# A recorded program becomes a graph that a list scheduler emits; maximum of x and part of a leaky rectifier go to ScalarE

## The chip, the cores and the metric

The kernel runs on one core of a Trainium2 chip. The metric is the device time of one execution in microseconds (us), the median of several; lower is better. Engines are named as in the profile: PE (TensorE matmul), PEld (its weight loads), DVE (VectorE), ACT (ScalarE), POOL (GpSimd), SP (SyncE, which issues DMAs). A name with a q is an engine's DMA queue or sequencer.

## What is computed

Four stages in a row, all in float32 accuracy:

```python
scores = q @ k^T / 8 - log(448)              # 4 batches x 12 heads, 448 positions, 64 wide
x   = sigmoid(scores) @ v                    # then heads side by side: 1792 tokens x 768
h   = x @ w_in;  g = h - tanh(h)             # layer 1, 768 -> 2048
x2  = g @ w_out                              # layer 2, 2048 -> 768
h2  = x2 @ w_in2                             # layer 3, 768 -> 2048
g2  = max(h2, 0) + alpha * min(h2, 0)        # leaky rectifier, alpha per column
out = g2 @ w_out2                            # layer 4, 2048 -> 768
```

## The kernel before

**Matmuls.** Every float32 operand is split into two float16 halves, high and low (`hi = f16(x*s)`, `lo = f16(x*s - hi)`); a product is three passes, hi*hi, hi*lo, lo*hi. All matmuls have 448 columns. The tokens are in two halves (`sb` 0 and 1) of 896. The attention runs in 12 groups `g`; each has seven units `u` of scores (`scores`) and seven of values (`values`, float32 matmuls), the values two steps behind the scores. Layers 1 and 2 (`product`) have 1152 matmuls of 128x128x448 each; layer 1 visits `sb` 0 four columns ahead of `sb` 1. Layers 3 and 4 use seven products in place of eight (`SEQ = (1, 2, 6, 5, 7, 4, 3)`, Strassen-like sums of blocks) and have 1008 matmuls each, 504 for a half. In layer 3 each half has four rounds `q`, each of seven units of 18 matmuls (`matmuls_in`).

**Buffers.** 51 slots of 128x896 float32 in SBUF are taken and given back by `alloc` and `release`, the longest free one first. PSUM has four tiles of two banks, ps0 to ps3. In the attention ps0 to ps2 go round for scores and ps3 collects the values. Layers 1 and 2 go round all four. In layer 3, products 1, 6, 7 and 4 gather in ps0 or ps1 (by round), product 2 in ps2, products 5 and 3 in ps3; what stands in ps0 or ps1 is copied out after product 1, after 6 and after 7, and read by the rectifier after 4.

**Side work.** Each of the weights' 64 units (768 columns) comes from HBM as 64-bit words into one of four staging tiles (POOL queue), three DVE instructions make float32 of it (`words`), layers 3 and 4 add and subtract blocks (`quarter`), the halves are made (`halves_of`: high on ACT or DVE, low on DVE), and a POOL-queue DMA stores them to scratch in HBM (`to_scratch`). SP fetches them from there when they are near their use. Between layers a scale is found: a maximum over a tile (`absmax` for x on DVE; from layer 1 on ACT sums squares), over the partitions on POOL, then seven small DVE instructions (`scale_jobs`), and the activations are split with it (`split_job`, `in_jobs`, `out_jobs`).

**What sets the order.** The program is emitted in the order in which the Python runs, and each engine executes its own instructions in that order. The class `Engine` keeps a rough clock per engine; `bg` pops jobs (or a step of the weights' conversion) into the DVE and ACT streams while DVE's clock is behind PE's. A low half is kept back until the next `settle`. The rectifier of layer 3 is `finish`: DVE adds the PSUM tile to the copy, two DVE `tensor_scalar` make `alpha*min`, one DVE instruction adds `max`, ACT squares the result with a running sum. Product 4 (`tail_in`) uses two ACT Relus and two DVE instructions instead.

Of the kernel before, what the change touches and what calls it, by code (L numbers as in the profile page):

```python
# [19 lines left out]
T2 = 2 * S  # L34
# [3 lines left out]
UN = 6  # L38
NU = KD * KF // UN

# [7 lines left out]
DEPTH = 5  # L48
# [6 lines left out]
LAG = 4  # L55


class Engine:
# [3 lines left out]
    def __init__(self, tc, raw, pe=None):  # L62
        self.tc, self.raw, self.pe, self.t = tc, raw, pe, 0.0

    def __getattr__(self, op):
        f = getattr(self.raw, op)

        def call(*args, **kw):
            if "dma" in op or op in ("memset", "partition_all_reduce"):
                return self.tc.keep_in_program_order(f(*args, **kw))  # L70
            out, args = args[0], args[1:]
            used = [a for a in (out, *args) if hasattr(a, "space")]
            n = int(np.prod((args[0] if op == "tensor_reduce" else out).shape[1:]))
            if op == "matmul":
                part = args[0].shape[0] * args[0].shape[1] / 16384
                self.t += part * n * (1.68e-3 if args[0].dtype == F32 else 0.421e-3) + (0.01 if part < 1 else 0.0)
            else:
                if any(a.space == bass.MemoryType.PSUM for a in used):
                    self.t = max(self.t, self.pe.t)
                    rate = 1.04e-3  # L80
                else:
                    rate = 0.52e-3 if op == "tensor_scalar" else 1.04e-3
                self.t += n * (0.83e-3 if op == "activation" else rate) + (0.26 if op == "activation" else 0.16)
            return self.tc.keep_in_program_order(f(out, *args, **kw))  # L84

        return call
# [3 lines left out]
def body(ctx: ExitStack, tc, qkd, vd, w1, w2, w3, w4, al, out):  # L90
    nc = tc.nc
    PE = Engine(tc, nc.tensor)
    V, A = Engine(tc, nc.vector, PE), Engine(tc, nc.scalar, PE)
    G, SP = Engine(tc, nc.gpsimd), Engine(tc, nc.sync)
# [5 lines left out]
    scratch = {(m, pr, q): dr_pool.tile([128, 2 * UN * 128], F16, name=f"scr{m}_{pr}_{q}")  # L100
               for m in (2, 3) for pr in range(1, 8) for q in range(NQ)}
    scratch.update({u: dr_pool.tile([128, 2 * UN * 128], F16, name=f"scr_{u}") for u in range(2 * NU)})
    slots = [sb_pool.tile([128, T2], F32, name=f"slot{i}") for i in range(NSLOT)]
    stage = [sb_pool.tile([128, UN * 128, 2], I32, name=f"stage{i}") for i in range(NSTAGE)]
# [4 lines left out]
    sc = sb_pool.tile([128, 8, 8], F32, name="sc")  # L109
    sci = sc.bitcast(I32)  # L110
    pst = [ps_pool.tile([128, 2, 512], F32, name=f"ps{i}") for i in range(4)]

    free = list(slots)

    def alloc():
        return free.pop(0)

    def release(t):
        free.append(t)
# [6 lines left out]


    wd = (w1, w2, w3, w4)
    wslot = {}
    loaded = [0]  # L130

    def load_unit(queue=G):
        i = loaded[0]
        if i < 4 * NU:
            src = wd[i // NU][i % NU].bitcast(I32)
            queue.dma_start(out=stage[i % NSTAGE].rearrange("p a b -> p (a b)"), in_=src)
            loaded[0] += 1

    def words(i, w):
        st = stage[i % NSTAGE]  # L140
        lo, hi = st[:, :, 0], st[:, :, 1]
        V.tensor_scalar(w, hi, 3, 0x3FFFFFFF, ALU.logical_shift_left, ALU.bitwise_and)
        yield
        V.scalar_tensor_tensor(w, hi, -0x40000000, w, ALU.bitwise_and, ALU.bitwise_or)
        yield
        V.scalar_tensor_tensor(w, lo, 29, w, ALU.logical_shift_right, ALU.bitwise_or)
        load_unit()
        yield

    def pair_of(s):  # L150
        return s.bitcast(F16)[:, 0:2 * UN * 128].rearrange("p (a c) -> p a c", a=2)

    late = []

    def settle():
        while late:
            late.pop(0)()

    def halves_of(hi, lo, src, scale, then):

        def low():
            V.scalar_tensor_tensor(lo, src, scale, hi, ALU.mult, ALU.subtract)
            then()

        if V.t + 0.4 < A.t:
            V.tensor_scalar(hi, src, scale, None, ALU.mult)
        else:
            A.activation(hi, src, AF.Copy, scale=scale)
        settle()
        late.append(low)  # L170

    def to_scratch(key, src, scale, then):
        t = alloc()
        v = pair_of(t)

        def stored():
            G.dma_start(out=scratch[key], in_=t.bitcast(F16)[:, 0:2 * UN * 128])
            release(t)
            then()

        halves_of(v[:, 0], v[:, 1], src, scale, stored)

    def counted(w):
        def f():
            release(w)
            nconv[0] += 1
        return f

    def conv():
        for i in range(2 * NU):  # L190
            w = alloc()
            yield from words(i, w.bitcast(I32)[:, 0:UN * 128])
            to_scratch(i, w[:, 0:UN * 128], SW, counted(w))
            yield
        for m in (2, 3):
            for q in range(NQ):
                yield from quarter(m, q)


    def quarter(m, q):  # L200
        def unit(b):
            s = alloc()
            yield from words(NU * m + 4 * q + b, s.bitcast(I32)[:, 0:UN * 128])
            f.append(s)

        def fl(s):
            return s[:, 0:UN * 128]

        def put(pr, s, last, scale=SW2):
            to_scratch((m, pr, q), fl(s), scale, lambda: release(s) if last else None)  # L210

        f = []
        yield from unit(0)
        yield from unit(1)
        a21, a22 = f
        r = alloc()
        V.tensor_tensor(fl(r), fl(a21), fl(a22), ALU.add)
        yield
        put(5, r, False)
        yield  # L220
        put(4, a22, True, -SW2)
        yield
        yield from unit(2)
        a11 = f[2]
        V.tensor_tensor(fl(r), fl(r), fl(a11), ALU.subtract)
        yield
        put(6, r, False)
        V.tensor_tensor(fl(a21), fl(a11), fl(a21), ALU.subtract)
        yield
        put(7, a21, True)  # L230
        yield
        put(1, a11, True)
        yield
        yield from unit(3)
        a12 = f[3]
        V.tensor_tensor(fl(r), fl(a12), fl(r), ALU.subtract)
        yield
        put(3, r, True)
        yield
        put(2, a12, True)  # L240
        yield
        settle()
        prepared.add((m, q))
        nconv[0] += 4

    prepared = set()
    nconv = [0]
    conv_gen = conv()
    reserve = [0]

    def conv_step(force=False):
        if nconv[0] >= 4 * NU or (not force and len(free) <= reserve[0]):
            return False
        next(conv_gen, None)
        V.t += 0.06
        return True

    def weight(m, n):
        load_units(m * NU + n // UN + 1)
        v = wslot[m, n // UN].bitcast(F16)[:, 0:2 * UN * 128]  # L260
        return v.rearrange("p (a k c) -> p a k c", a=2, k=UN)[:, :, n % UN, :]

    taken = [0]

    def load_units(upto):
        while taken[0] < min(upto, 3 * NU):
            i = taken[0]
            src = i if i < 2 * NU else i - NU
            while nconv[0] <= src:
                settle() if late else conv_step(True)  # L270
            t = alloc()
            SP.dma_start(out=t.bitcast(F16)[:, 0:2 * UN * 128], in_=scratch[src])
            wslot[divmod(i, NU)] = t
            taken[0] += 1

    jobs = []
# [10 lines left out]
    def flush():  # L287
        while jobs:
            jobs.pop(0)()

    def scale_jobs(g, n, f0=1.0, f1=1.0, root=None, exp=ACT_EXP, sw=SW):
        c = sc[:, g]
        ci = sci[:, g]

        def first():
            V.tensor_reduce(c[:, 0:1], mx[:, g, 0:n], AX.X, ALU.max)
            G.partition_all_reduce(c[:, 1:2], c[:, 0:1], 128, bass_isa.ReduceOp.max)  # L300
            return 0.1

        def second():
# [11 lines left out]
            return 0.5  # L315

        return first, second

    def unit_jobs(g):

        c, ci = sc[:, g], sci[:, g]
# [660 lines left out]
```

## Time and profile before

| what | value |
|---|---|
| runs: median (lowest to highest of 3) | 985.47 us (983.61 to 986.0) |
| the profiled execution: span, first to last instruction | 981.4 us; of its own time only this span is given |
| PE busy | 948.3 us |
| DVE, ACT, POOL busy | 772.2, 512.8, 84.9 us |
| matmuls | 5280, of them 4320 in the layers |

A row of the timeline reads: start, time covered, engine, line, operation, out<-in, count, and in brackets the idle time before and what ended it. In the kernel before, all engines' instructions have line 84 and POOL's DMAs line 70, since a helper records them, so rows are told apart by names and shapes: `slot` an SBUF slot, `ps` a PSUM tile, `sc` the scales, `stage` the staging tiles, `scr` scratch in HBM. A stretch's row gives its length and each engine's busy time and count, the granted TensorE clock (1.00 is 2.4 GHz, 0.50 is 1.2 GHz), the DMA share and GB/s.

### The profile page before, as it was taken

Reading aid. Unit: us, or ns where it says so; the run is one execution under the profiler, and the core shown is the slowest. Engines: PE = TensorE matmul, PEld = TensorE weight load, DVE = VectorE, ACT = ScalarE, POOL = GpSimd, SP = SyncE. Lnnn points to the kernel's source line nnn. Section 1 sums busy time; section 2 is a strip of 40 time slices with the busy share of each in tenths; the row PEclk is TensorE's granted clock in tenths of the full one; section 3 lists DMA queues with packets and bytes.
Section 4 is the critical chain, followed back from the end, with each engine's and each line's share of the span. In section 5 each row is a group of like instructions: output and inputs, shape, how many; then the busy total and the mean of one; then the engine's idle time right before and its main releaser. Section 6 shows DMA issues by size and latency. Waiting matters only on the chain. (4 is left out here: it accounts for less than half of the span.)

```text
span 981.4 us, 13376 instructions
## 1 busy us (share of the span) xinstructions
PE 948.3 (97%) x5280; PEld 465.3 (47%) x5280; DVE 772.2 (79%) x949; ACT 512.8 (52%) x628; POOL 84.9 (9%) x163
## 2 busy tenths in 40 slices
PE   7999999999999999999999978999999899999998
PEld 2333345555555544555555534455445454545554
DVE  4988879999988988878999998998864549756810
ACT  6667768999889976423524234333333424503400
POOL 0110100100000001112123210010100000000000
PEclk9999999999999999999999998999999999999999
DMA  9962443443321025698469993566552324344621
GB/s 355 350 249 92 162 145 114 140 150 129 129 97 49 1 65 191 217 334 322 175 225 342 330 365 105 161 213 221 183 172 67 110 81 162 109 147 147 221 74 59
DMA packets 48286, 170.75 MB, mean 174 GB/s; under 512 B 6112, under 2 KB 9440, under 8 KB 48224
## 3 DMA queue, kind: packets, MB, share of 16 engines
q1 hardware_dynamic: 32544, 88.10, 26.7%
q0 software_dynamic: 15680, 81.80, 22.9%
q8 instruction: 41, 0.67, 0.3%
q14 instruction: 21, 0.17, 0.1%
HBM read 129.77 MB, written 40.11 MB: 173 GB/s over the span
## 5 line engine op out<-in xcount | busy, mean ns | idle before, releaser
L84 PE MATMUL ps<-slot,slot 128*128 128x448 f16 (+2 forms) x4704 | 895.8, 370 | 23.9 <-DVE slot L84 13.2
L84 PEld LDWEIGHTS <-slot 128*128 128x128 f16 (+2 forms) x4896 | 445.2, 98 | 473.0 <-issue 62.6
L84 ACT ACTIVATE slot<-slot 128x896 f32<-128x896 f32 (+3 forms) x127 | 112.5, 897 | 205.1 <-DVE slot L84 171.2
L84 ACT ACTIVATE slot<-slot,sc 128x896 f16<-128x896 f32 (+1 forms) x155 | 154.3, 1029 | 106.4 <-DVE slot L84 95.9
L84 DVE SCALAR_TENSOR_TENSOR slot<-slot,slot 128x768 f16<-128x768 f32 (+3 forms) x137 | 135.5, 996 | 21.4 <-ACT slot L84 19.5
L84 DVE SCALAR_TENSOR_TENSOR slot<-slot,sc,slot 128x896 f16<-128x896 f32 (+1 forms) x122 | 135.2, 1138 | 5.7 <-ACT slot L84 5.2
L84 DVE SCALAR_TENSOR_TENSOR slot<-stage,slot 128x768 int32<-128x768 int32 x128 | 122.6, 958 | 3.5
L84 DVE SCALAR_TENSOR_TENSOR slot<-ps,sc,slot 128x896 f32<-128x896 f32 (+1 forms) x50 | 48.3, 979 | 89.1 <-PE ps L84 57.5
L84 ACT ACTIVATE slot<-ps,cst 128x896 f32<-128x896 f32 x84 | 79.5, 1006 | 37.9 <-PE ps L84 37.8
L70 POOL DMA_DIRECT2D scr<-slot x88 | 48.1, 546 | 354.7 <-DVE slot L84 286.0
L84 ACT ACTIVATE slot<-ps,sc 128x896 f32<-128x896 f32 (+1 forms) x56 | 47.1, 841 | 60.1 <-PE ps L84 60.1
L84 DVE TENSOR_TENSOR slot<-slot,slot 128x768 f32<-128x768 f32 (+2 forms) x82 | 76.3, 932 | 1.4
L84 ACT ACTIVATE slot<-slot,cst 128x896 f32<-128x896 f32 x64 | 66.7, 1042 | 2.2
L84 ACT ACTIVATE slot<-ps 128x896 f32<-128x896 f32 x52 | 46.2, 905 | 38.0 <-PE ps L84 38.0
L84 PE MATMUL ps<-slot 64*128 64x448 f16 (+1 forms) x576 | 57.1, 358 | 5.1 <-DVE slot L84 5.1
L70 POOL DMA_DIRECT2D stage<-w x60 | 33.8, 564 | 216.8 <-DVE slot L84 216.7
L84 DVE TENSOR_SCALAR slot<-stage 128x768 int32<-128x768 int32 x64 | 35.6, 556 | 10.2 <-DMA scr<-slot 7.2
L84 DVE TENSOR_TENSOR slot<-ps,slot 128x896 f32<-128x896 f32 x24 | 26.1, 1087 | 21.3 <-ACT slot L84 20.0
L84 DVE COPY_PREDICATED slot<-slot,ps 128x896 f32<-128x896 int32 x32 | 38.1, 1191 | 1.1
L84 DVE SCALAR_TENSOR_TENSOR slot<-slot,ps 128x896 f32<-128x896 f32 x32 | 34.6, 1080 | 5.2 <-ACT slot L84 5.0
L84 PEld LDWEIGHTS ps<-slot,slot 128*64 128x64 f32 (+1 forms) x384 | 20.1, 135 | 38.6 <-issue 37.1
L84 DVE SCALAR_TENSOR_TENSOR ps<-ps,sc,slot 128x896 f32<-128x896 f32 x32 | 36.9, 1152 | 0.0
(23 smaller groups left out, 148.9 us busy)
## 6 DMA issues: line engine op xcount, KB each, us to landing
slot<-scr SPq DMA_DIRECT2D x160, 384.0 KB, 3.8
stage<-w POOLq DMA_DIRECT2D x60, 768.0 KB, 5.5
scr<-slot POOLq DMA_DIRECT2D x88, 384.0 KB, 4.3
slot<-qk SPq DMA_DIRECT2D x23, 448.0 KB, 8.0
slot<-v SPq DMA_DIRECT2D x12, 448.0 KB, 7.5
out_t<-slot SPq DMA_DIRECT2D x24, 224.0 KB, 2.0
stage<-w SPq DMA_DIRECT2D x4, 768.0 KB, 10.8
slot<-qk SPq DMA_DIRECT2D x2, 224.0 KB, 2.6
```

The source lines that it names most:

```text
L70: return self.tc.keep_in_program_order(f(*args, **kw))
L84: return self.tc.keep_in_program_order(f(out, *args, **kw))
```

## The change

The helper with the clocks and the job lists go. Every piece of work becomes a node of a `Plan` with its engine (or a choice, "AV": ACT or DVE), a cost per engine, what it reads and writes, and the code that emits it. `deadlines` walks back from the end and gives each node the latest time at which it may end; `run` then plays the engines forward in time and on each engine emits the ready node with the earliest deadline. PE's nodes keep the order in which they were added. A node that needs a new slot waits until enough are free, and takes the one with the lowest number; a fetch of weights may not be emitted more than 18 us ahead of need. A DMA is reckoned as 0.8 us, 1/0.33 us per MB in a single line, and 1.2 us.

Two pieces of arithmetic move. The values of a group are copied from ps3 by ACT instead of DVE, and x's maximum by DVE (12 reductions) becomes a sum of squares by ACT (12 instructions with a running sum, into a tile `junk`), from which a square root gives the scale. In layer 3's `finish` ACT makes `relu(-h)` and `relu(h)`, and two DVE instructions add `-alpha*relu(-h)`; the two `tensor_scalar` and the `max` instruction on DVE go.

PE's instructions are the same ones in the same order. DVE has 42 fewer rows of work in the printed order, ACT 98 more.

```diff
-    def bg(lead=0.0, most=1.0):
-        while max(V.t, A.t - most) < PE.t + lead:
-            if jobs:
-                jobs.pop(0)()
-            elif not conv_step():
-                V.t = max(V.t, PE.t + lead - 2.0)
-                return
...
+    def deadlines(self):
+        total = sum(n.cost["T"] for n in self.nodes if n.engine == "T")
+        for n in reversed(self.nodes):
+            length = min(n.cost.values())
+            ends = [a.late - (0.0 if n.engine == "T" and a.engine == "T" else n.lat) for a in n.after]
+            n.late = min(ends, default=total + 8.0) - length - (n.cost.get("M", 0.0) * self.MB)
...
+                for n in waiting[e]:
+                    if n.ready > now + 1e-9 or n in begun:
+                        continue
+                    slack = n.late - base
+                    if n.window is not None and slack > n.window:
+                        continue
+                    key = n.late + (6.0 if len(n.engine) > 1 and e == "V" else 0.0)
...
+            if "M" in n.cost:
+                moved = max(moved, now + 0.8) + n.cost["M"] * self.MB
+                n.end = moved + 1.2
+            n.emit(e)
...
+        add("AV", {"A": act(n, ptr=ptr), "V": vec(n, ptr, True)}, high, [*reads, *extra],
+            [(dst, "h", r) for r in regions], keep=keep)
+        add("V", {"V": vec(n, ptr)}, low, [*reads, *extra, *((dst, "h", r) for r in regions)],
+            [(dst, "l", r) for r in regions])
...
-            V.tensor_copy(two(x[j, b]), p[:, :, 0:S])
-            absmax(x[j, b], b // 2, 2 * j + b % 2)
+            add("A", {"A": act(T2, True)}, lambda e: A.activation(two(slot(name)), full(3), AF.Copy),
+                banks(3), whole(name))
+            add("A", {"A": act(T2, acc=True)},
+                lambda e: A.activation(junk, slot(name), AF.Square, scale=SQ,
+                                       accum_out=mx[:, b // 2, col:col + 1]),
+                whole(name), [("junk",), (f"mx{b // 2}", col)])
...
         def finish(sb, i, j, q, p, t, col):
-            V.tensor_tensor(two(t), p[:, :, 0:S], two(t), ALU.add)
-            n = alloc()
-            for k in range(2):
-                f = 2 * q + k + i * KF // 2
-                V.tensor_scalar(two(n)[:, k], two(t)[:, k], 0.0, alpha[:, f:f + 1], ALU.min, ALU.mult)
-            V.scalar_tensor_tensor(t, t, 0.0, n, ALU.max, ALU.add)
-            A.activation(n, t, AF.Square, scale=SQ, accum_out=mx[:, 6 + sb, col:col + 1])
+        add("V", {"V": vec(T2)}, lambda e: V.tensor_tensor(two(slot(a)), full(k0), two(slot(a)), ALU.add),
+            banks(k0), whole(a))
+        add("A", {"A": act(T2)}, lambda e: A.activation(slot(b), slot(a), AF.Relu, scale=-1.0), whole(a), whole(b))
+        add("A", {"A": act(T2)}, lambda e: A.activation(slot(a), slot(a), AF.Relu), (), whole(a))
+        leak(a, b, 2 * q + i * KF // 2)
+        squares(a, b, 6 + sb, col)
...
+    def leak(a, b, f0):
+        for k in range(2):
+            add("V", {"V": vec(S, 1)},
+                lambda e, k=k: V.scalar_tensor_tensor(two(slot(a))[:, k], two(slot(b))[:, k],
+                                                      nalpha[:, f0 + k:f0 + k + 1], two(slot(a))[:, k],
+                                                      ALU.mult, ALU.add),
+                [(b, k), ("nalpha",)], [(a, k)])
```

Three places of the order, before and after. **The start of the attention on ACT.** `cst` in a row marks a sigmoid that empties a PSUM tile; the other rows with 128x448 and 128x896 make high halves of q and k. Before:

```order
L84 ACTIVATE slot_157<-slot_151 128x448
L84 ACTIVATE slot_158<-ps_211,cst 128x896
L84 ACTIVATE slot_159<-ps_212,cst 128x896
L84 ACTIVATE slot_163<-ps_213,cst 128x896
L84 ACTIVATE slot_164<-ps_211,cst 128x896
```

After:

```order
L210 ACTIVATE slot_171<-slot_151 128x448 x2
L210 ACTIVATE slot_151<-slot_152 128x896
L210 ACTIVATE slot_172<-ps_212,cst 128x896
L210 ACTIVATE slot_173<-ps_213,cst 128x896
L210 ACTIVATE slot_152<-ps_214,cst 128x896
```

ACT now makes the high half of the second pair too (`slot_151<-slot_152`), ahead of the first sigmoid.

**The first round of layer 3 on ACT.** `ps_214,mx` (before) and `ps_215,mx` (after) are the sum of squares of layer 2's last tile, rows with `sc` are high halves of layer 3's operands, a row `slot,mx<-slot` is the sum of squares that ends a `finish`, and `slot<-ps_211` (before) and `slot<-ps_212` (after) are copies of ps0 after products 1, 6 and 7. Before:

```order
L84 ACTIVATE ps_214,mx<-ps_214 128x2x448
L84 ACTIVATE slot_173<-ps_211 128x896
L84 ACTIVATE slot_178<-slot_186,sc 128x896
L84 ACTIVATE slot_168,mx<-slot_173 128x896
L84 ACTIVATE slot_163<-ps_211 128x896
L84 ACTIVATE slot_198<-ps_211 128x896
L84 ACTIVATE slot_183,mx<-slot_198 128x896
```

After:

```order
L210 ACTIVATE ps_215,mx<-ps_215 128x2x448
L210 ACTIVATE slot_164<-ps_212 128x896
L210 ACTIVATE slot_183<-slot_166,sc 128x896
L210 ACTIVATE slot_185<-slot_189,sc 128x896
L210 ACTIVATE slot_186<-slot_193,sc 128x896
L210 ACTIVATE slot_191<-slot_179,sc 128x896
L210 ACTIVATE slot_192<-slot_195,sc 128x896
L210 ACTIVATE slot_165<-ps_212 128x896
L210 ACTIVATE slot_161<-slot_170,sc 128x896
```

The second copy of ps0 stood behind the `finish` of product 2 (`slot_168,mx<-slot_173`, which waits for DVE); now five high halves stand there, and that `finish` comes after the copy.

**The passage from layer 3 to layer 4 on DVE.** `slot<-ps` is a `finish`'s addition, `TENSOR_REDUCE` begins the scale of the second half (`sb` 1), rows with two `sc` operands (`slot_160<-slot_187,sc,slot_160`) are low halves for layer 4. Before, from the last `finish` on:

```order
L84 TENSOR_TENSOR slot_152<-ps_214,slot_152 128x896
L84 TENSOR_SCALAR slot_176<-slot_152,alpha 128x448 x2
L84 SCALAR_TENSOR_TENSOR slot_152<-slot_152,slot_176 128x896
L84 TENSOR_REDUCE sc<-mx 128x1
L84 TENSOR_SCALAR sc<-sc 128x1 x7
L84 SCALAR_TENSOR_TENSOR slot_160<-slot_187,sc,slot_160 128x896
L84 SCALAR_TENSOR_TENSOR slot_186<-slot_151,sc,slot_186 128x896
L84 SCALAR_TENSOR_TENSOR slot_170<-slot_200,sc,slot_170 128x896
```

After, in the second half's first round, some 430 matmuls of PE's order earlier (here `TENSOR_REDUCE` begins the scale of the first half, `sb` 0):

```order
L210 TENSOR_REDUCE sc<-mx 128x1
L210 TENSOR_SCALAR sc<-sc 128x1 x7
L210 TENSOR_SCALAR slot_177<-slot_152,sc 128x896
L210 TENSOR_SCALAR slot_180<-slot_175,sc 128x896
L210 SCALAR_TENSOR_TENSOR slot_176<-slot_164,sc,slot_176 128x896
L210 SCALAR_TENSOR_TENSOR slot_177<-slot_152,sc,slot_177 128x896
L210 TENSOR_TENSOR slot_151<-ps_215,slot_151 128x896
L210 SCALAR_TENSOR_TENSOR slot_180<-slot_175,sc,slot_180 128x896
L210 SCALAR_TENSOR_TENSOR slot_181<-slot_160,sc,slot_181 128x896
```

The four operands of layer 4's first product (`sb` 0) are split right after their scale, not behind the scale of the other half.

## Rows read from the trace of the kernel before

**Rows 1.** The page, part 1: busy time, share and instructions of each engine.

```profile
PE 948.3 (97%) x5280; PEld 465.3 (47%) x5280; DVE 772.2 (79%) x949; ACT 512.8 (52%) x628; POOL 84.9 (9%) x163
```

**Rows 2.** Stretches: attention, layers 1 to 4, and two short ones after waits.

```profile
0.00:130.10 130.10, 124.98 (x960) 41.94 (x960) 103.18 (x133) 87.26 (x94) 11.37 (x25) 1.00 0.67 244
130.10:348.10 218.00, 218.00 (x1157) 112.80 (x1154) 203.57 (x227) 193.66 (x225) 15.31 (x29) 1.00 0.29 98
348.10:569.50 221.40, 218.43 (x1153) 112.64 (x1152) 193.01 (x238) 92.96 (x121) 43.04 (x80) 1.00 0.72 254
569.50:784.70 215.20, 197.47 (x1029) 100.82 (x1027) 165.98 (x243) 80.92 (x122) 15.19 (x29) 0.98 0.51 172
784.70:981.40 196.70, 189.41 (x989) 97.13 (x988) 106.50 (x111) 58.04 (x68) 0.00 (x0) 0.99 0.36 125
...
592.00:595.00 3.00, 2.97 (x9) 1.26 (x9) 3.00 (x5) 0.00 (x0) 0.00 (x0) 0.53 0.81 280
785.98:789.39 3.41, 3.41 (x11) 1.37 (x10) 3.41 (x4) 1.36 (x2) 0.00 (x0) 0.50 0.00 0
```

**Rows 3.** Timeline of PE alone, layers 2 to 4, runs that follow a wait.

```profile
361.79 1.59 PE L84 MATMUL ps<-slot,slot 128*128 128x448 f16 x6 [0.73 <-DVE slot L84]
...
592.03 8.15 PE L84 MATMUL ps<-slot,slot 128*128 128x448 f16 x35 [7.17 <-ACT slot L84]
...
718.35 51.24 PE L84 MATMUL ps<-slot,slot 128*128 128x448 f16 x270 [0.29 <-ACT slot L84]
770.59 10.56 PE L84 MATMUL ps<-slot,slot 128*128 128x448 f16 x55 [1.00 <-ACT slot L84]
784.75 29.09 PE L84 MATMUL ps<-slot,slot 128*128 128x448 f16 x144 [3.60 <-DVE slot L84]
...
974.90 2.43 PE L84 MATMUL ps<-slot,slot 128*128 128x448 f16 x12 [0.78 <-DVE slot L84]
```

**Rows 4.** Timeline of ACT at the start of layer 3.

```profile
590.13 0.95 ACT L84 ACTIVATE slot<-slot 128x896 f32<-128x896 f32 x1 [3.66 <-DVE slot L84]
```

**Rows 5.** Groups by shape: count, busy us, mean ns of one, idle before.

```profile
L84 ACT ACTIVATE slot<-ps,cst 128x896 f32<-128x896 f32 x84 | 79.5, 1006 | 37.9 <-PE ps L84 37.8
...
L84 ACT ACTIVATE slot<-slot 128x896 f32<-128x896 f32 x64 | 60.8, 950 | 87.0 <-DVE slot L84 86.0
...
L84 ACT ACTIVATE slot<-ps 128x896 f32<-128x896 f32 x52 | 46.2, 905 | 38.0 <-PE ps L84 38.0
...
L84 DVE SCALAR_TENSOR_TENSOR slot<-slot,slot 128x896 f32<-128x896 f32 x24 | 26.2, 1093 | 0.8
...
L84 DVE TENSOR_SCALAR slot<-slot,alpha 128x448 f32<-128x448 f32 x48 | 19.6, 450 | 0.9
...
L84 DVE COPY slot<-ps 128x896 f32<-128x896 f32 x12 | 13.1, 1091 | 11.2 <-PE ps L84 11.2
L84 DVE TENSOR_REDUCE mx<-slot 128x1 f32<-128x896 f32 x12 | 13.0, 1086 | 0.4
...
L84 DVE SCALAR_TENSOR_TENSOR slot<-slot,nalpha,slot 128x448 f32<-128x448 f32 x16 | 10.2, 681 | 18.4 <-ACT slot L84 18.4
...
L84 ACT ACTIVATION_READ_ACCUMULATOR slot<-slot 128x1 f32 x32 | 6.0, 187 | 0.0
```

**Rows 6.** Timeline of the first 12 us: second pair's split, scores, sigmoids, values.

```profile
7.19 0.63 DVE L84 TENSOR_SCALAR slot<-slot 128x896 f16<-128x896 f32 x1 [1.80 <-DMA slot<-qk]
...
8.99 2.41 PE L84 MATMUL ps<-slot 64*128 64x448 f16 x28 [0.75 <-DVE slot L84]
...
9.59 3.70 ACT L84 ACTIVATE slot<-ps,cst 128x896 f32<-128x896 f32 x4 [0.48 <-PE ps L84]
...
11.34 1.72 PE L84 MATMUL ps<-slot,slot 128*64 128x448 f32 x8
```

**Rows 7.** DMA issues: KB each, median us to landing; fetches at layer 3's end.

```profile
scr<-slot POOLq DMA_DIRECT2D x88, 384.0 KB, 4.3
...
DMA to landing us min/median/max: 2.8/3.0/4.4
```

More of the change, by code (lines that the diff above doesn't have):

```diff
@@ L55, with __init__ @@
 LAG = 4
[L58 to L63 removed]
+PASSES = ((0, 0), (0, 1), (1, 0))
+SEQ = (1, 2, 6, 5, 7, 4, 3)
+class Node:
+    def __init__(self, n, engine, cost, emit, reads, writes, lat, window, keep):
+        self.n, self.engine, self.cost, self.emit = n, engine, cost, emit
+        self.touched = list(dict.fromkeys(r[0] for r in (*reads, *writes)))
+        self.lat, self.window, self.keep = lat, window, keep
+        self.before, self.after = set(), []
+        self.late = self.end = None
+        self.left, self.ready = 0, 0.0
@@ L65, in __getattr__, with __init__ @@
+class Kept:
+    def __init__(self, tc, raw):
+        self.tc, self.raw = tc, raw
     def __getattr__(self, op):
         f = getattr(self.raw, op)
[L68 to L84, printed above, removed]
@@ L109, in body @@
     sc = sb_pool.tile([128, 8, 8], F32, name="sc")
+    junk = sb_pool.tile([128, T2], F16, name="junk")
     sci = sc.bitcast(I32)
     pst = [ps_pool.tile([128, 2, 512], F32, name=f"ps{i}") for i in range(4)]
[L113 to L119, printed above, removed]
+    add = plan.add
     def two(t):
@@ L125, in hl, with slot, whole @@
         return t.bitcast(F16).rearrange("p (a t) -> p a t", a=2)
-    wd = (w1, w2, w3, w4)
[L129 to L139, printed above, removed]
+    def slot(name):
+        return plan.slot(name)
+    def whole(name):
+        return [(name, 0), (name, 1)]
@@ L172, in to_scratch @@
[L172 to L197, printed above, removed]
@@ L287, in flush, with w @@
[L287 to L303, printed above, removed]
+        def w():
+            return slot(name).bitcast(I32)[:, 0:UC]
+        s = [(f"#stage{i % NSTAGE}",)]
@@ new lines, in body, with fetch, scale_of, second @@
+    fetched = [0]
+    def fetch(key, name):
+        add("S", {"S": 0.06, "M": 0.393},
+            lambda e: SP.dma_start(out=slot(name).bitcast(F16)[:, 0:2 * UC], in_=scratch[key]),
+            [("#scr", key)], [(name, 0)], window=18.0, keep=6.0)
+    def scale_of(g, n, f0=1.0, f1=1.0, root=None, exp=ACT_EXP, sw=SW, unit=False, reads=()):
+        c, ci = sc[:, g], sci[:, g]
+        add("V", {"V": 0.16}, lambda e: V.tensor_reduce(c[:, 0:1], mx[:, g, 0:n], AX.X, ALU.max),
+            [(f"mx{g}", k) for k in range(n)], [(f"#sm{g}",)])
+        add("G", {"G": 0.4}, lambda e: G.partition_all_reduce(c[:, 1:2], c[:, 0:1], 128, bass_isa.ReduceOp.max),
+            [(f"#sm{g}",)], [(f"#sa{g}",)], lat=0.3)
+        def second(e):
@@ new lines, in body, with need @@
+    for each in todo:
+        values_of(*each)
+    for i in range(NU, 2 * NU):
+        convert(i)
+    for sb in range(2):
+        scale_of(sb, KD, root=SQ, unit=True)
+        for j in range(KD // 2):
+            for b in range(2 * sb, 2 * sb + 2):
+                split_act(f"sX{j},{b}", f"sx{j},{b}", sb)
+    got = set()
+    def need(m, n0, nk):
+        for u in weight_units(m, n0, nk):
+            if (m, u) not in got:
+                got.add((m, u))
+                fetch_units(m, u, False)
```

1153 lines of the change are left out of this document (559 added, 594 removed).

## Prediction

> **What bounds the kernel now.** I read the busy shares first [rows 1]: PE works 948.3 of 981.4 us, so a shorter DVE or ACT pays only where PE waits for it. Then one row for each stage [rows 2]: the length of a stretch less PE's busy time is PE's idle time there. It is 5.1 us in the attention, none in layer 1, 3.0 at the passage from layer 1 to layer 2, 17.7 in layer 3 with both its passages, 7.3 in layer 4. The last matmul ends at 974.90 + 2.43 = 977.33, so 4.1 of layer 4's idle time is the tail behind PE, and 3.2 lie inside. Last I read PE's own timeline [rows 3], where a row ends at a wait and the brackets name who ended it. From the first such row of the layers (361.79) to the last (974.90) there are 17 waits, together 23.9 us (3.0 + 17.7 + 3.2).
>
> How fast would PE be without them? The difference of two undisturbed runs of matmuls gives the pace: (51.24 - 10.56) / (270 - 55) = 0.1892 us each [rows 3]. At that pace a run of 12 needs 2.27 and its row says 2.43, so each run also has 0.16 us at its end. The 4320 matmuls of the layers need 817.3 us, and they take 977.33 - 130.10 = 847.2. The excess is 29.9, in three terms: 23.9 of waits; 17 x 0.16 = 2.7 of ends; and half-clock stretches behind the two longest waits. After the 7.17 the granted clock was 0.53 for 3.00 us, after the 3.60 it was 0.50 for 3.41 us [rows 2], which costs 3.00 x 0.47 + 3.41 x 0.50 = 3.1. The sum is 29.7. I can thus name nearly all that can be won with PE's instructions unchanged: 30 us, 3%.
>
> **What the change removes.** The largest wait shows what causes them. ACT's square of a `finish` waits 3.66 us for DVE and runs from 590.13 for 0.95 [rows 4]; the copy of ps0 right behind it takes 0.905 [rows 5], and 590.13 + 0.95 + 0.905 = 591.99, when PE, which needs ps0 empty, starts again (592.03). The copy itself waited for nothing but its place in ACT's order. The second listing shows it moved ahead of that square. The 3.60 before 784.75 has the same form on DVE: a low half of layer 4's first operand behind the last `finish` and a whole scale. The third listing shows it now some 430 matmuls earlier, 430 x 0.189 = 81 us. The other waits of layer 3 are copies behind squares (released by ACT) or low halves held back (by DVE), the 3.0 before layer 2 low halves of g. In the changed order each piece of these stands ahead of the side work that delayed it, with one exception: the 1.00 at 770.59, in the last round, where product 4 follows product 7 in the same PSUM tile with only ACT's copy between. That copy's length stays, so 1.0 + 0.16 = 1.2 remains of the 29.9. **Gain: -28.7.**
>
> **What the moved arithmetic costs.** DVE loses 12 copies and 12 maxima, 12 x (1.091 + 1.086) = 26.1, and in 24 finishes 24 x (2 x 0.450 + 1.093) = 47.8; it gains 48 of the instructions with `nalpha`, 48 x 0.681 = 32.7 [rows 5]. Net it is 41 us lighter. ACT gains 12 x (0.905 + 0.950 + 0.187) = 24.5 and two Relus per finish; the nearest row is the 0.950 of the same shape and types, so 24 x 1.90 = 45.6. In layer 3 ACT was busy for 80.9 of 215.2 [rows 2] and has the room. In the attention it was busy for 87.3 of 130.1; 11 of the 12 copies and squares lie there (+22.5), and the order gives it some more high halves (up to two a group), so 115 to 120 of 130. On average PE (125.0 / 12 = 10.4 us a group) still covers that: cost 0, and a rival below.
>
> A rule speaks against this move. By the Trainium skill (ScalarE: Activation LUTs, Rules for kernel authors) relu, max, add and multiply belong on VectorE, up to about three times as fast per element in bf16. The rows here show float32: 2 x 0.450 on DVE against 0.950 for one such pass on ACT, about equal. By the rule the two Relus would waste some 30 us of engine time, but that enters the sum only where PE waits for ACT.
>
> **The start.** Before, DVE splits the second pair at 7.19, when it has landed, for 0.63; ACT goes from sigmoid to sigmoid [rows 6]. Now ACT makes that high half ahead of its first sigmoid (first listing). If the landing stays, ACT is free at 7.19 + 0.95 = 8.14; four sigmoids at 3.70 / 4 = 0.925 end at 11.84; they free the PSUM tile that the seventh unit of scores waits for, and a unit is 8 matmuls at 2.41 / 28, 0.69. The values start at 12.5 in place of 11.34. PE never gets this back. **Cost: +1.2** (bounds: 0 if the scheduler's other choices absorb it, 2 if a sigmoid more is late).
>
> **New waits.** The scheduler fetches at most 18 us ahead; in layer 3's last round some fetches lead by 18 to 35 matmuls, 3.4 to 6.6 us, against landings of 3.0, at most 4.4 [rows 7]. That is 0 to 1.0 for one of them. Other small waits must come, since the plan's clock is not the chip's: between 0 and half of what stood there, I take **+1.5**, about what two of the seven short waits of layer 3's rounds cost.
>
> **Sum.** 981.4 - 28.7 + 1.2 + 1.5 = 955.4 for the span. The median of the runs is 985.47, 4.1 above the span; that difference I keep, **959.5 us**, 2.6% less.
>
> **Rivals.**
>
> *ACT becomes the bound in the attention, or a good part of the small waits returns.* A group with two splits on ACT asks for 7 x 1.006 + 0.905 + 0.950 + 0.187 + 2 x 0.950 = 11.0 us [rows 5] against PE's 10.4. At 0.6 in each of 12 groups that is +7.2: 966.7. If half of the 23.9 of waits also stays, it would be 959.5 + 12 = 971.5 by itself. For it: ACT at about 90% of the attention. Against: the sigmoids stand 0.925 apart in a row, not 1.006, and few groups have two splits.
>
> *The change does not do what its order says.* If the latenesses are of chip times that no order mends, the waits come back elsewhere: 985.5 + 1.2 = about 986. Against: the two largest waits end on work that was ready long before.
>
> *Slower: DVE is held by slots that are not free yet.* A slot was given out after the longest rest; now the lowest number goes, so a slot just given back is written again at once. The two scratch stores of a weights' unit land 4.3 after issue [rows 7]; the plan reckons 0.8 + 0.393 MB / 0.33 + 1.2 = 3.2. If the next instruction on DVE or ACT wants that slot, it waits, and all that stands behind it in that engine's order waits too, low halves for PE among them. At 1.1 for each of two stores that is 2.2 a unit. About 47 units are converted in layers 1 and 2, where DVE has 218.0 - 203.6 + 221.4 - 193.0 = 43 us to spare [rows 2]. So it decides from (43 + 26) / 47 = 1.5 us a unit on, where the whole gain is gone; at 2.2 it gives 959.5 + 47 x 2.2 - 43 = 1020. Against: there are 51 slots, not all in use, and half a unit's time is enough to land.
>
> **How the numbers follow.** The forecast holds with 0.62; ACT as the bound or half of the waits back 0.24; no gain 0.05; held DVE 0.09. The range for 8 in 10: down to 955.5, where no start cost and only 1.2 of residual waits and fetches together are met (959.5 - 1.2 - 1.5 = 956.8) and the 1.2 at 770.59 goes as well; up to 973, which takes in the second case's 971.5 with the start at its worse bound. A measurement of this kernel can tell about 0.3% (3 us) from no change. Faster by more: forecast and second case, 0.86; within: 0.05; slower: the held DVE, 0.09.
>
> **What would show it.** PE's timeline of the layers should have one wait near 1.0 us in the last round of layer 3 and few others, none over 2, and no granted clock of half speed after the start. In the passage to layer 3, the copy of ps0 should run as soon as product 1 ends. The stretch of layers 3 and 4 should be shorter by some 23 us, layers 1 and 2 by 3, the attention longer by 1. DVE should be down by about 40 us, ACT up by 70. The forecast is wrong if ACT shows no idle time in the attention while PE waits for ACT, or if DVE's idle time in layers 1 and 2 is released by DMA on slots, or if the waits at 580 to 592 and 781 to 785 stand where they were.

## The result, and the profile after

The changed kernel takes 961.59 us (median of 4 executions, 957.92 to 963.32) against 985.33 (983.61 to 986.0): the ratio is 0.9752, interval 0.9728 to 0.9776. Five more rounds later gave 960.43 against 984.23, ratio 0.9765 (0.9740 to 0.9791). The profiled execution has a span of 955.9 us and a time of 957.92.

The busy shares of the changed kernel (page, part 1; before: [rows 1]) and its stretches, attention and layers 1 to 4 (columns as in [rows 2]: length, then busy time and count of PE, PEld, DVE, ACT, POOL, granted clock, DMA share, GB/s):

```profile
PE 943.6 (99%) x5280; PEld 464.7 (49%) x5280; DVE 708.7 (74%) x878; ACT 593.0 (62%) x739; POOL 87.6 (9%) x163
```

```profile
0.00:131.26 131.26, 125.28 (x961) 42.16 (x961) 100.01 (x133) 111.24 (x135) 17.45 (x36) 1.00 0.76 278
131.26:349.57 218.31, 218.09 (x1157) 112.73 (x1154) 203.79 (x233) 199.75 (x238) 19.58 (x37) 1.00 0.38 130
349.57:567.48 217.91, 217.91 (x1152) 112.71 (x1152) 195.27 (x250) 96.58 (x125) 44.23 (x78) 1.00 0.69 247
567.48:760.96 193.48, 191.46 (x1009) 98.60 (x1008) 113.27 (x153) 115.03 (x155) 5.96 (x11) 1.00 0.41 133
760.96:955.90 194.94, 190.85 (x1009) 98.53 (x1007) 96.37 (x113) 70.43 (x89) 0.35 (x1) 1.00 0.43 136
```

Each stretch here starts with the first matmul of its layer. PE's idle time (length less busy time) is 2.0 us in layer 3, 0.2 at the passage to layer 2 and none inside layer 4, whose 4.1 are the tail behind PE. The half-clock stretches of [rows 2] are gone. PE's own timeline says the same, four waits in the layers in place of 17 ([rows 3]):

```profile
349.57 252.35 PE L210 MATMUL ps<-slot,slot 128*128 128x448 f16 x1332 [0.21 <-ACT slot L210]
602.45 10.52 PE L210 MATMUL ps<-slot,slot 128*128 128x448 f16 x54 [0.53 <-DVE slot L210]
613.39 139.76 PE L210 MATMUL ps<-slot,slot 128*128 128x448 f16 x738 [0.42 <-ACT slot L210]
754.16 197.65 PE L210 MATMUL ps<-slot,slot 128*128 128x448 f16 x1044 [1.01 <-ACT slot L210]
```

The last of them, 1.01, is the structural one in the last round of layer 3 that the prediction kept. Where 7.17 us were lost before, ACT's timeline now shows the second copy of ps0 at 580.39, between high halves and with no idle time before it; in [rows 4] it came behind a square that had waited 3.66 for DVE.

```profile
575.71 4.78 ACT L210 ACTIVATE slot<-slot,sc 128x896 f16<-128x896 f32 x5 [2.90 <-DVE sc L210]
580.39 0.89 ACT L210 ACTIVATE slot<-ps 128x896 f32<-128x896 f32 x1
```

In sum the 4320 matmuls of the layers go from 847.2 to 951.81 - 131.26 = 820.55 us, 26.7 less, and the attention ends 1.2 later.

Something new stands in the list of waits of the changed kernel (engine, line, what it waited for: us in total, times, longest):

```profile
ACT slot L210 <- DMA scr<-slot: 26.3, 13, 11.2
DVE slot L210 <- DMA scr<-slot: 8.2, 7, 3.6
```

ACT and DVE stood still for 34.5 us until a store to scratch had read the slot that they were to write. Before it was 13.2:

```profile
DVE slot L84 <- DMA scr<-slot: 7.2, 2, 4.1
ACT slot L84 <- DMA scr<-slot: 6.0, 2, 5.2
```

Little of it reaches PE in this execution, but the chain is there:

```profile
612.42 0.92 ACT L210 ACTIVATE slot<-ps 128x896 f32<-128x896 f32 x1 [1.43 <-DMA scr<-slot]
```

A copy out of PSUM came 1.43 late because its slot was still being stored, and PE waited 0.42 for that copy (613.39 above).

### The profile page after: what moved, and what is told of

It reads as the page before. It is cut to its first block, busy times and chain, and to the rows that moved or that the text cites. A ratio compares the mean times of both kernels' runs of the same rounds, so it can differ in the third digit from the quotient of the medians.

```text
span 955.9 us, 13508 instructions
## 1 busy us (share of the span) xinstructions
PE 943.6 (99%) x5280; PEld 464.7 (49%) x5280; DVE 708.7 (74%) x878; ACT 593.0 (62%) x739; POOL 87.6 (9%) x163
## 5 line engine op out<-in xcount | busy, mean ns | idle before, releaser
L210 ACT ACTIVATE slot<-slot 128x896 f32<-128x896 f32 (+3 forms) x193 | 171.9, 903 | 141.0 <-DVE slot L210 103.9
L210 ACT ACTIVATE slot<-slot,sc 128x896 f16<-128x896 f32 (+1 forms) x164 | 164.0, 1030 | 61.2 <-PE ps L210 23.8
L210 DVE SCALAR_TENSOR_TENSOR slot<-slot,sc,slot 128x896 f16<-128x896 f32 (+1 forms) x122 | 132.6, 1138 | 5.6 <-ACT slot L210 5.4
L210 DVE SCALAR_TENSOR_TENSOR slot<-slot,slot 128x768 f16<-128x768 f32 (+2 forms) x113 | 108.9, 977 | 30.4 <-ACT slot L210 28.5
L210 ACT ACTIVATE slot<-ps 128x896 f32<-128x896 f32 x64 | 57.4, 909 | 62.1 <-PE ps L210 42.2
L210 DVE TENSOR_TENSOR slot<-slot,slot 128x768 f32<-128x768 f32 (+2 forms) x82 | 73.9, 933 | 10.0 <-ACT slot L210 9.7
L210 DVE SCALAR_TENSOR_TENSOR slot<-slot,nalpha,slot 128x448 f32<-128x448 f32 x64 | 41.0, 681 | 40.0 <-ACT slot L210 40.0
```

The source lines that it names most:

```text
L210: return lambda *args, **kw: self.tc.keep_in_program_order(f(*args, **kw))
```

## The experiments

My theory: nearly all of the gain comes from the order, which the deadlines make, and the moved arithmetic adds nothing by itself. The main rival: a DVE that is 41 us lighter lets go of PE. A second question, from the new waits, was what the reuse of slots costs.

**The arithmetic alone.** The kernel before, its job lists untouched:

```diff
-            V.tensor_copy(two(x[j, b]), p[:, :, 0:S])
-            absmax(x[j, b], b // 2, 2 * j + b % 2)
+            A.activation(two(x[j, b]), p[:, :, 0:S], AF.Copy)
+            A.activation(junk, x[j, b], AF.Square, scale=SQ, accum_out=...)
...
-                V.tensor_scalar(two(n)[:, k], two(t)[:, k], 0.0, alpha[:, f:f + 1], ALU.min, ALU.mult)
-            V.scalar_tensor_tensor(t, t, 0.0, n, ALU.max, ALU.add)
+            A.activation(n, t, AF.Relu, scale=-1.0)
+            A.activation(t, t, AF.Relu)
+            # then two scalar_tensor_tensor with nalpha on DVE
```

> The kernel before, with the moved arithmetic alone: x copied by ACT, its squares summed by ACT, the two Relus of layer 3's finish on ACT; job lists and order as before. Theory (the order makes the waits): PE's large waits at the passages stay, 978 to 992 us, 985 likeliest, since the finish's chain now passes through ACT twice and the copy of ps0 still stands behind the square. Rival (a lighter DVE makes the gain): waits shrink as DVE loses 41 us, 962 to 970 us.

It took 990.66 us, ratio 1.0064 (1.0045 to 1.0082): slower by 5.4, though DVE is busy for 734.5 us in place of 772.2. The attention ends at 130.19, as before. The layers take 8.0 us more. ACT's timeline at the start of layer 3 tells why:

```profile
582.42 1.93 ACT L84 ACTIVATE slot<-slot 128x896 f32<-128x896 f32 x2 [1.63 <-DVE slot L84]
585.76 0.95 ACT L84 ACTIVATE slot<-slot 128x896 f32<-128x896 f32 x1 [1.41 <-DVE slot L84]
586.61 0.19 ACT L84 ACTIVATION_READ_ACCUMULATOR slot<-slot 128x1 f32 x1
586.71 0.90 ACT L84 ACTIVATE slot<-ps 128x896 f32<-128x896 f32 x1
```

The finish now crosses from DVE to ACT to DVE to ACT, and the copy of ps0 still comes last; PE goes on at 587.65, when it ends. (PE's row names a DMA as what ended that wait of 4.24, but the copy ends at 587.61; the name is that of the event which came last.) Other waits grew, as 6.26 in place of 3.60 at the passage to layer 4. In the old order the arithmetic is a loss.

**The order alone.** The changed kernel with the old arithmetic as nodes of its graph (copy, maximum, two `tensor_scalar` and the `max` instruction on DVE, the edits above undone).

> The changed kernel with the old arithmetic put back into its graph: x copied and its maximum taken on DVE, the finish with two tensor_scalar and a max instruction on DVE. Theory (order): within 4 us of the changed kernel, 958 to 966 us, DVE 41 us busier and hidden. Rival (arithmetic): 972 to 985 us, with waits on DVE in layers 1 to 3.

It took 962.37 us, ratio 0.9771 (0.9748 to 0.9793), as fast as the changed kernel, with DVE busy for 734.9 and ACT for 542.3. Its layers take 820.63 us, the changed kernel's 820.55. The graph and its scheduler make the gain. (The choice of engine for high halves and the slots are the scheduler's too; they are not told apart from the order here.) Its attention is 5.1 us longer, by waits of 1.86 and 1.06 on DVE's copy of ps3 and by a stretch at half clock in the start:

```profile
11.43:14.84 3.41, 3.41 (x22) 1.10 (x22) 2.58 (x4) 3.41 (x4) 0.00 (x0) 0.50 1.02 416
```

The copy behind the wait of 1.86 was late because the DVE instruction ahead of it had waited for a store:

```profile
107.44 0.56 DVE L210 TENSOR_SCALAR slot<-stage 128x768 int32<-128x768 int32 x1 [2.13 <-DMA scr<-slot]
```

**One move by hand.** The kernel before, with the square of a finish put off until after the next copy:

```diff
-            A.activation(n, t, AF.Square, scale=SQ, accum_out=mx[:, 6 + sb, col:col + 1])
-            release(n)
+            squares.append(square)
...
             A.activation(two(t), p[:, :, 0:S], AF.Copy)
+            while squares:
+                squares.pop(0)()
```

> The kernel before with one hand move: the square that ends a finish in layer 3 is written after the next copy of a PSUM tile on ACT, not before it. Theory: the 7.17 us wait, its half-clock stretch (1.4) and the short waits that ACT ended (about 1.1 together) go, the others stay: 974 to 978 us. Rival (the wait only changes its name, because DVE is late): 983 to 987 us.

It took 979.89 us, ratio 0.9945 (0.9929 to 0.9962). That is 5.3 us less and lies between the two expectations. PE's timeline:

```profile
587.49 20.59 PE L84 MATMUL ps<-slot,slot 128*128 128x448 f16 x108 [2.48 <-ACT slot L84]
610.63 96.92 PE L84 MATMUL ps<-slot,slot 128*128 128x448 f16 x504 [2.55 <-DVE slot L84]
...
775.62 0.53 PE L84 MATMUL ps<-slot,slot 128*128 128x448 f16 x1 [5.17 <-ACT slot L84]
777.65 32.34 PE L84 MATMUL ps<-slot,slot 128*128 128x448 f16 x162 [1.50 <-DVE slot L84]
```

The 7.17 fell to 2.48, because the copy now stands behind a high half that itself waits for DVE. Of the seven short waits in the rounds, 4.7 us together, two are left, the 2.55 (0.46 before) and one of 0.29; the square's place in ACT's order cost most of the others. But in the last round the put-off squares pile up ahead of the scale, and the 3.60 became 5.17 + 1.50. One fixed rule for a piece helps in one place and harms in another.

**The scheduler without deadlines.**

```diff
-                    key = n.late + (6.0 if len(n.engine) > 1 and e == "V" else 0.0)
+                    key = n.n + (0.0 if len(n.engine) > 1 and e == "V" else 0.0)
```

> The changed kernel with its list scheduler, but among the ready pieces of an engine the one that was added first goes first, in place of the one with the earliest deadline. Theory (the deadlines do it): conversions of weights, added ahead of a layer, go ahead of what PE waits for in it; slower than before, 1000 us or more, with waits in layers 1 to 3 ended by DVE. Rival (playing the engines forward is enough): within 5 us of the changed kernel, 957 to 967 us.

It took 1033.34 us, ratio 1.0502 (1.0474 to 1.0530), with six waits in layer 1 (34.6 us together) and one of 10.65 in layer 3, all ended by DVE; layer 2 has none. The last two of layer 1:

```profile
225.79 132.22 PE L210 MATMUL ps<-slot,slot 128*128 128x448 f16 x684 [7.25 <-DVE slot L210]
370.04 370.35 PE L210 MATMUL ps<-slot,slot 128*128 128x448 f16 x1944 [12.03 <-DVE slot L210]
```

```profile
354.00 12.83 DVE L210 SCALAR_TENSOR_TENSOR slot<-slot,sc,slot 128x896 f16<-128x896 f32 x12
```

Before the first of the six (8.08) DVE made conversions of weights between other pieces, as theory said. During the longest it made low halves of activations, sixteen in a row (the row shows twelve), and before the 10.65 fourteen sums of blocks: all of it work that had been added to the graph earlier. The same graph and the same emission forward in time lose 72 us with this key. So playing the engines forward is not enough. The edit also takes out the 6 us by which DVE leaves a piece to ACT, and the two were not run apart; that the deadlines are the larger part I argue from the low halves and the sums, which are DVE's alone.

**The changed kernel again**, as the base of the next three.

> The changed kernel unedited, as the base of the three runs beside it. Its four executions so far spread from 957.9 to 963.3 us, their mean granted clock from 1.000 to 0.997. Theory A (a half-clock stretch in the start, in some executions): spread again 957 to 964; an execution with a mean clock near 0.998 is about 2 us longer than one with 1.000, and a profile with such a stretch has it in its first 20 us. Rival B (a late fetch or store somewhere in the layers): the stretch stands behind a wait in layers 1 to 4.

It took 959.69 to 965.13, median 960.43. The two longest executions (963.23 and 965.13) have mean granted clocks of 0.997 and 0.996, the others 0.999 or 1.000. That fits stretches at half clock, but their places are not known. The profiled execution (959.97, mean clock 1.000) has no such stretch on record, yet its matmuls show one in the start:

```profile
9.58 4.20 PE L210 MATMUL ps<-slot 64*128 64x448 f16 x30 [1.51 <-ACT slot L210]
13.72 1.72 PE L210 MATMUL ps<-slot,slot 128*64 128x448 f32 x8
```

Here 30 matmuls of the scores take 4.20 us, where 28 took 2.41 in the kernel before [rows 6]. Most of them start in pairs 0.37 us apart, the same as in the stretch of granted clock 0.50 of the second experiment, and 0.19 apart in the first profile of this kernel. The values start at 13.72 in place of 12.48, and the attention ends at 132.49, 1.2 later. So theory A's stretch is there, and the mean clock does not tell it. The profile also has a wait of 1.37 at the start of layer 2, as rival B would; its layers take 821.42 us. What makes the two longest executions longer stays open.

**The start put back.** The high half of the second pair tied to DVE (`on="V"` for pair 1).

> The changed kernel with the high half of the second pair tied to DVE, as before the change. Forecast of the term: the first values at 11.3 in place of 12.5 us in the profile, and 1.2 us less in all, 959 to 961.5 us. Rival (the start is bound by landings or the clock, not by ACT): values still at 12 or later, no change beyond 0.5 us.

It took 965.07 us (961.44 to 968.13), 4.6 more than its base, so the expectation failed. The values start at 13.60, not at 11.3, as the rival said, because the matmuls ahead of them ran at half pace as in the base:

```profile
9.30 4.38 PE L210 MATMUL ps<-slot 64*128 64x448 f16 x28 [0.57 <-DVE slot L210]
```

So this run does not tell what the tie is worth. The larger loss lies elsewhere: the attention ends at 139.40. In the reshuffled order the copy of the values out of ps3 stood still:

```profile
130.38 0.92 ACT L210 ACTIVATE slot<-ps 128x896 f32<-128x896 f32 x1 [5.88 <-DMA scr<-slot]
```

```profile
131.35 3.26 PE L210 MATMUL ps<-slot,slot 128*64 128x448 f32 x8 [4.03 <-ACT slot L210]
```

```profile
129.54:136.36 6.82, 5.00 (x14) 1.72 (x16) 4.87 (x6) 4.77 (x7) 1.61 (x3) 0.50 0.93 357
```

ACT waited 5.88 us for a store to leave the slot that it had been given, and PE waited 4.03 for ACT. The granted clock was 0.50 for 6.82 us from within that wait on; eight matmuls then took 3.26 us, where a full clock runs them in 1.72. This is the mechanism of the prediction's slower rival, on ACT.

**A longer lead for fetches.** `window=18.0` made 40.0.

> The changed kernel with the limit on how far ahead weights are fetched raised from 18 to 40 us. If fetches are what PE waits for in the longer executions (rival B): 957 to 959 us and a spread under 2 us. If not (theory A): 960 to 963, the same spread, within 1 us of the unedited kernel.

It took 1007.08 us, 47 more than its base: a miss for both sides. PE waited 16.73, 11.04 and 12.76 us in layer 4:

```profile
804.78 9.74 PE L210 MATMUL ps<-slot,slot 128*128 128x448 f16 x36 [16.73 <-DMA slot<-scr]
825.56 9.59 PE L210 MATMUL ps<-slot,slot 128*128 128x448 f16 x36 [11.04 <-DMA slot<-scr]
```

The fetches are late because what they fetch is not written: DVE's last conversions of weights out of the staging tiles (count, ns, then the first and last start) run up to 827 us, in the changed kernel up to 593. First this kernel, then the changed one:

```profile
L210 DVE SCALAR_TENSOR_TENSOR slot<-stage,slot x128: 936/952/971, 35.2 to 827.3; 128x768 int32<-128x768 int32 x128
```

```profile
L210 DVE SCALAR_TENSOR_TENSOR slot<-stage,slot x128: 934/957/974, 34.7 to 592.7; 128x768 int32<-128x768 int32 x128
```

By the scheduler's code a conversion starts only while several slots are free, and weights fetched early hold them. That the fetches took exactly those slots I argue from the code; it was not counted. The limit of 18 us is worth more than it seems.

**The longest free slot first.**

```diff
-                    k = min((f for f in self.free if f[0] <= now + 1e-9), key=lambda f: f[1])
+                    k = min((f for f in self.free if f[0] <= now + 1e-9), key=lambda f: f[0])
```

> The changed kernel with the longest free slot taken first in place of the one with the lowest number. The rival of the prediction (engines held by slots whose stores land late) would show: 2 us or more faster, less idle time of DVE and ACT released by DMA. My reading (slots rest long enough): within 1 us of the unedited kernel.

It took 956.28 us (954.91 to 957.26), ratio to before 0.9709 (0.9685 to 0.9732), 4.2 less than its base, and no execution has a mean clock under 1.000. In the profiles 2.9 of this lie in the layers; the attention ends 1.4 earlier, because the values start at 12.28 and the base's profile had the slow start. The list of waits has no row for a store to scratch. Of the four waits in the layers one is left:

```profile
751.95 197.65 PE L210 MATMUL ps<-slot,slot 128*128 128x448 f16 x1044 [1.00 <-ACT slot L210]
```

Its layers take 949.60 - 131.06 = 818.54 us; 4320 at 0.1892 with the 1.2 that stays would be 818.5. My reading that slots rest long enough was wrong.

**The lowest slot, but a truer store.** The plan reckons a store 2.0 us longer:

```diff
-                n.end = moved + 1.2
+                n.end = moved + 1.2 + n.cost.get("L", 0.0)
```

> The changed kernel, still giving out the slot with the lowest number, but its plan reckons a store to scratch 2.0 us longer, 5.2 in place of 3.2 (the profile's median to landing is 5.1), before the slot is free. If the wrong estimate of the store is what the lowest number needs to do harm: ACT's and DVE's idle time released by stores falls from 34 us to under 10, and the time to 956 to 958 us. Rival (only the rest of a slot counts, since stores land up to 10 us and more late): it falls by less than half, 959 to 962 us.

It took 956.64 us, ratio 0.9700 (0.9671 to 0.9730), and the waits on stores fell from 34.5 us to this one row:

```profile
DVE slot L210 <- DMA scr<-slot: 0.2, 1, 0.2
```

So it is the plan's estimate that does the harm: 3.2 us where a store takes 5.1 in the median of the changed kernel's profile. The lowest number only makes it show. Either remedy is enough.

**The longest free slot with the old arithmetic.**

> The longest free slot first, and the old arithmetic in the graph (x copied and its maximum on DVE, the finish with two tensor_scalar and a max instruction on DVE). Theory (the moved arithmetic is worth nothing by itself): within 1.5 us of the kernel with the longest free slot alone, 955 to 958 us. Rival (DVE needs the 41 us): 959 to 964 us, with waits on DVE that no store released.

It took 959.91 us, ratio 0.9734 (0.9705 to 0.9763), 3.6 more than with the new arithmetic. The two ran in different rounds; against the kernel before in the same rounds the difference is 0.0025 of the time, 2.5 us, and the intervals overlap. That is about the rival's time, by another way. Its one new wait in the layers is not on DVE:

```profile
751.65 3.58 PE L210 MATMUL ps<-slot,slot 128*128 128x448 f16 x18 [2.50 <-DMA slot<-scr]
```

A fetch in the last round of layer 3 is late, as in the second experiment at the same place (1.92). It costs 2.7 with its end. The attention ends 1.6 later: 1.3 of it is the slow start again (values at 13.62 in place of 12.28), which the new arithmetic had in the changed kernel's second profile too, and 0.2 a wait for DVE's copy of ps3. So the old arithmetic is not faster under the scheduler, but that DVE's time is the reason is not shown. Why the fetch is late is left open.

**The best, with two small terms.** The longest free slot first, the second pair's high half on DVE, and the copy after product 7 in the last round cut into two banks, one on ACT, one on DVE.

> The longest free slot first, with the high half of the second pair tied to DVE, and in layer 3's last round the copy after product 7 cut in two, one bank on ACT, one on DVE, product 4 in two halves. If the two terms are real: values start at 11.3 us (1.2 less) and the wait of 1.0 in the last round of layer 3 falls to about 0.5, in all 954 to 955 us. Rival (the start gives nothing back, and tying the half to DVE costs elsewhere): 956 us or more.

It took 955.45 us (954.50 to 955.67), ratio to before 0.9687 (0.9658 to 0.9716), the fastest of all, by 0.8 us over the longest free slot alone, within what the two can tell. The start gives 0.35: the attention ends at 130.71 in place of 131.06, the values start at 11.94 in place of 12.28. They would start at 11.3, as expected, had the matmuls ahead of them not run at half pace in part, 28 of them in 3.05 us in place of 2.41 [rows 6]:

```profile
8.96 3.05 PE L210 MATMUL ps<-slot 64*128 64x448 f16 x28 [0.50 <-DVE slot L210]
```

The cut copy gives nothing: PE waits 1.29 in place of 1.00, as the two halves ran one behind the other,

```profile
750.63 1.35 ACT L210 ACTIVATE slot<-ps 128x448 f32<-128x448 f32 x2 [2.49 <-PE ps L210]
```

```profile
751.20 0.63 DVE L210 COPY slot<-ps 128x448 f32<-128x448 f32 x1 [9.70 <-ACT slot L210]
```

DVE started its half at 751.20, released by ACT's, which had begun 0.57 before: by the row it was a dependency in the program that held it, so two copies side by side were not tried.

**More work for ACT in the attention.** The longest free slot first, all high halves of q and k from the third pair on tied to ACT.

> The longest free slot first, and every high half of q and k from the third pair on tied to ACT: 23 of them on ACT in the attention in place of 7. By the prediction's rival (a group asks ACT for 11.0 us, 7 sigmoids at 1.006): attention longer by up to 7 us, 960 to 964 us, ACT without idle time there. By the busy time per sigmoid, 79.5 / 84 = 0.946, a group asks for 10.6: 956 to 959 us.

It took 957.27 us, 1.0 more than without, within what runs of different rounds can tell. ACT is busy for 120.6 of 133.0 us, and PE waits for it nowhere behind the start. The attention of the profiled execution is 2.0 longer, of which 1.7 is a stretch of the start at half clock:

```profile
0.00:133.04 133.04, 126.55 (x960) 42.32 (x961) 86.67 (x116) 120.64 (x148) 15.24 (x34) 0.99 0.75 279
11.00:14.40 3.40, 3.36 (x24) 0.97 (x21) 1.09 (x1) 3.40 (x5) 0.00 (x0) 0.50 1.03 417
```

## Why the prediction was right, step by step

**What can be won.** The prediction named 29.7 us of excess in the layers and kept 1.2. With the slots mended the layers take 818.54 us, 28.7 less than 847.2, which is the gain as forecast; without that the changed kernel has 26.7, where the sum has 28.7 - 1.5 = 27.2. The waits, their ends and the half-clock stretches were counted rightly, and the stretches followed the waits away. The gain of the changed kernel also lay where the prediction put it: layers 3 and 4 shorter by 23.4 (207.8 to 193.5, and 199.9 to 190.8), layers 1 and 2 by 3.2.

**That the order does it.** Shown by two runs in opposite directions: the order without the arithmetic has the whole gain in the layers (820.63 against 820.55), the arithmetic without the order loses 5.4. Within what the scheduler sets, the deadlines are the part that was tried, together with the 6 us of the engine choice: 72 us lost without them. That the 7.17 was the copy's place behind the square is shown by the changed order and in part by the hand move, which took 4.7 of it.

**The moved arithmetic at zero.** Right for the time: with and without it the layers of the changed kernel take the same. In the attention the old arithmetic lets PE wait 3.1 us for DVE's copies, 0.2 with the longest free slot. DVE fell by 63.5 us where 41 was worked out, ACT rose by 80 where 70 was. What I hadn't followed through is the choice of engine for high halves: DVE makes 27 fewer, 15.6 us by the groups of the two profiles, and ACT makes them. The rest of the difference is not placed. By the Trainium skill (ScalarE: Activation LUTs, Rules for kernel authors) relu, max and add belong on VectorE. Here, in float32, giving them back to DVE under the same scheduler brought nothing: 962.37 against 961.59, and 959.91 against 956.28 with the longest free slot. Both engines have idle time in this kernel.

**The start.** Forecast: values at 12.5, 1.2 lost. The profile has them at 12.48, and the attention ends 1.16 later.

```profile
7.20 0.95 ACT L210 ACTIVATE slot<-slot 128x896 f16<-128x896 f32 x1 [2.72 <-DMA slot<-qk]
...
12.48 1.72 PE L210 MATMUL ps<-slot,slot 128*64 128x448 f32 x8
```

That the number fits is in part luck. The forecast assumes full clock, and the second profile of the same kernel has the values at 13.72, behind matmuls at half pace; a stretch at half clock costs up to 1.7 us in the start (the second and the last experiment). The way back gave only 0.35, with half pace in part of its start; without the 0.64 us that this took, the values would start at 11.3, as the term says. That is an estimate; no run shows the 1.2 in the time.

**The residual 1.5.** The size was right in the profiled execution, 820.55 - 818.54 = 2.0, its cause was not. I put it down to the plan's clock in general, and priced the held slots as a rival of their own with a chance of 0.09. The runs show that the whole residual in the layers is the held slots: it went when the slots rested and when the store was reckoned longer. The argument that 51 slots would leave them time to land failed, because the lowest number can be a slot that was just given back; in 20 cases its store had not landed. The rival's price failed too, 2.2 us for each of 47 units on DVE. Its sign, DVE's idle time in layers 1 and 2 released by stores, stood at 5.2 us (7.2 before); ACT was the engine that was held, for 26.3 us in all and 21.5 in these layers. Of all this 2.0 us reach PE in the layers of the first profile, and 2.9 (821.42 - 818.54) in those of the second.

**ACT as the bound.** The rival asked 11.0 us of ACT a group. In the changed kernel ACT is busy for 111.2 us of the attention, under the 115 to 120 that I reckoned. With 120.6 us in 12 groups, 10.05 each, as in the last experiment, PE still does not wait. The sigmoid's mean of 1006 ns [rows 5] counts the overlap of neighbours twice; 79.5 / 84 = 0.946 was the figure to use.

**From span to time.** Forecast 955.4 and 959.5, measured 955.9 and 961.6. That the time came so near is in part luck. The executions of both kernels whose span is listed take 1.8 to 2.3 us more than their span; the rest of the 4.1 that I carried over stood there because the profiled execution of the kernel before was among its shorter ones. So was that of the changed kernel, whose median lies 3.7 above it, and the two cancel. Between the medians the gain is 23.7 us, where 26.0 was forecast.

## What to carry to other kernels

Where the bounding engine stands still, find the instruction that released it and ask what stood ahead of that in its own queue: here a copy with all its inputs ready lay behind work that was waiting, and the scheduler's order, without the moved arithmetic, gave 2.3%. A plan that reuses buffers must reckon the DMA that still reads them by its measured landing, or let buffers rest; short estimates cost 2 to 3 us here, and 4.03 us of PE at once where a reshuffle put a critical copy onto such a buffer. And a limit like the 18 us of lead can hold a balance that no line names: widening it cost 47 us.

## What was not expected of the hardware

Stores to scratch of 384 KB landed in 5.1 us in the median and kept ACT from a slot for up to 11.2 us. In the attention a wait of PE of 4.03 us went with 6.82 us at a granted clock of 0.50, while waits of 1.92 and 2.50 in the layers of two runs were each followed by 18 matmuls in 3.58 us, full pace. In the start the same kernel ran its score matmuls at full pace in one profile and at half pace in another whose clock is recorded as 1.00 throughout; this cost 1.2 us.
